# Building one-hot scatter matrices as 32-bit words in a graph propagation kernel

## The chip, the cores and the metric

The kernel runs on one core of a Trainium2 chip. The metric is the device time of one execution in microseconds (us), and the time of a kernel is the median of its runs. The engines are PE (matrix products, with its weight loads as PEld), DVE (elementwise work and reductions), ACT (copies and functions), POOL (here mostly gathers by index) and SP (which issues most of the copies between memory and the on-chip buffers).

## The reference

`x` has N = 10000 rows of D = 128 floats. There are E = 160000 edges with a source and a destination node each. Seven times, each node's row becomes the sum over its incoming edges of the source's row, with two factors per edge:

```python
h = x
toks = [x]
for _ in range(K):                                   # K = 7 hops
    msg = h[src] * deg_inv_sqrt[src, None] * deg_inv_sqrt[dst, None]
    h = _segment_sum(msg, dst, N)
    toks.append(h)
```

The eight rows of a node are then the tokens of one attention block (layer norm, attention with `wq`, `wk`, `wv`, `wo`, a residual and a softmax readout with `w_r`), which gives one row per node.

## The kernel before, in words

**How a hop is computed.** The nodes are cut into 79 blocks of 128 destinations. For each block the edges are placed in slots, and a hop is two matrix products with one-hot matrices: a *gather* product picks the source rows of the slots out of a table in SBUF, and a *scatter* product adds the slots up into the 128 destinations. The matrices of a block lie in one fp8 tile `w` of 128 partitions by (19 + 18) x 128 columns. Its first 19 x 128 = 2432 columns are the scatter half: 19 groups of 128 slots, where the column of the slot's destination has a 1. Its last 18 x 128 = 2304 columns are the gather half. The matrices are the same in all seven hops. They are made once, during hop 1, used there, and stored to memory (`gsd`); hops 2 to 7 load them again.

**The stages.** First all edges are read and ranked by counting with one-hot matrices (`pass_a`, `decode`). Then comes hop 1, which works on 20 *quads* of four blocks (the last has three). Around it run three generators: `place` for the next quad, `matrices` for this one, and `hop1` (with `block`) for the quad before. Then follow hops 2 to 7 (L654 to L705), and the attention at the end. Before the attention a count decides whether a slow path is needed.

**`place` (L371 to L457).** It handles a quad in two pairs of blocks. For each pair DVE makes a one-hot tile `oh` (L195, called at L379; two buffers), PE sums it up (`ur`, L383), ACT copies, PE adds prefixes (L389), and `rank` makes the product `ux` on DVE (L208), has PE sum it (L212, L213) and reduces to `rk` (L216). From `rk` come `rob` (L195, at L394) and two tiles `R` (L201), and PE multiplies `oh` and `R` to the slot table `tb` (L402), which ACT copies to `tbs`. DVE then makes `vo` and its largest values `ov` (L405, L407). After both pairs the table's source rows are written to memory as `srow` (L412), and the destinations come back, through small products (L416), as `dsl`: one number per partition, block and slot group, which is 1 plus the destination within the block, or 0 where a slot is empty (L420, an ACT copy from PSUM into f16). Some ten small integer instructions, two one-hot tiles `ohp` (L446), PE's products of them (L449), `lo` (L452), `oidx` (L455) and `Sov` (L456) deal with edges that found no slot.

**`matrices` (L459 to L480).** For each block of a quad, `row` issues a copy of one row of `srow` to all partitions (`rb`, L464 to L466, one buffer, on SP). DVE compares `rb` with the partition's number, which is the gather half (L473), and compares `dsl` with 1 to 128, which is the scatter half (L476): the `dsl` value is stretched over 128 columns, the numbers 1 to 128 (`iof1`, f16) over the 19 groups. The next row's copy is issued as soon as the gather half has read the buffer. Then SP stores `w` to `gsd` (L478). `w` comes from a pool of six buffers, so a new one has to wait until an earlier block's products have read theirs.

**`block` (L492 to L566).** For each pair of slot groups PE makes eight gather products (L541), ACT copies the result to an f16 tile `eb` (L544), and PE makes the scatter products into `acc` (L517). Two products take rows that POOL fetched by index (`og`, L488; products at L503, L530). At the end of a block DVE reduces `acc` to `s` (L532), copies the degree `indeg` (L595) and reduces `mx` (L597), ACT scales (L596, L571), and SP stores the token rows `tok` (L575).

**The order of the work.** In the hops each engine's instruction list is written by a scheduler that plans with costs of its own and moves instructions of the three generators past each other; on the chip each engine then runs its list strictly in order and waits for semaphores. So a change of one instruction can move others. The attention is scheduled by hand.

Of the kernel before, what the change touches and what calls it, by code (L numbers as in the profile page):

```python
# [7 lines left out]
F32 = mybir.dt.float32  # L8
F16 = mybir.dt.float16
BF16 = mybir.dt.bfloat16  # L10
F8 = mybir.dt.float8e4
I32 = mybir.dt.int32
AF = mybir.ActivationFunctionType
ALU = mybir.AluOpType
# [15 lines left out]
NJ = NG + NI  # L30
# [7 lines left out]
class Hops:  # L38
# [332 lines left out]
    def place(self, ts, got):  # L371

        tc, nc, V, A, T, G = self.tc, self.nc, self.nc.vector, self.nc.scalar, self.nc.tensor, self.nc.gpsimd
        wp, w1, n = self.bwp, self.bw1, len(ts)
# [34 lines left out]
        n, a, b = len(ts), ts[0], ts[-1] + 1  # L409
        msc = self.psm.tile([128, 128], F32, name="msc")  # L410

        nc.sync.dma_start(self.srow[a:b, :].rearrange("t (s r) -> s t r", r=CAP), tbs[:4 * NG, :n, 0:CAP])  # L412
        dsl = wp.tile([128, 4, NJ], F16, name="dsl")
        for g in range(n):
            for q in range(4):
                T.matmul(msc[32 * q:32 * q + 32, 32 + g * NJ:32 + (g + 1) * NJ], tbs[:, g, CAP:2 * CAP], self.esel[:, q, :],  # L416
                         start=True, stop=True, tile_position=(0, 32 * q))
                T.matmul(msc[32 * q:32 * q + 32, 16 + g * NI:16 + (g + 1) * NI], tbs[:, g, 0:CAP], self.esel[:, q, NG:],
                         start=True, stop=True, tile_position=(0, 32 * q))
        A.copy(dsl[:, :n, :], msc[:, 32:32 + n * NJ].rearrange("p (g j) -> p g j", j=NJ))  # L420
        V.tensor_scalar(self.oidx[:, a:b, :NI], msc[:, 16:16 + n * NI].rearrange("p (g i) -> p g i", i=NI), -1.0, 0.0, op0=ALU.add, op1=ALU.max)
        got.append(dsl)
        n = 4
# [30 lines left out]
        n = len(ts)  # L454
# [4 lines left out]
    def matrices(self, ts, dsl, W):  # L459

        nc, V = self.nc, self.nc.vector

        def row(t):
            rb = self.bw1.tile([128, 4 * NG * CAP], F16, name="rb")  # L464
            r1 = self.srow[t:t + 1, :]
            nc.sync.dma_start(rb, bass.AP(tensor=r1.tensor, offset=r1.offset, ap=[[0, 128], [1, 4 * NG * CAP]]))  # L466
            return rb

        rb = row(ts[0])
        yield  # L470
        for g, t in enumerate(ts):
            w = self.gsp.tile([128, (NJ + NG) * 128], F8, name="w")
            V.tensor_scalar(w[:, NJ * 128:], rb, self.pid1, None, op0=ALU.is_equal, saturate=False)  # L473
            if t != ts[-1]:
                rb = row(t + 1)
            V.tensor_tensor(w[:, :NJ * 128].rearrange("p (j d) -> p j d", d=128), dsl[:, g, :, None].to_broadcast([128, NJ, 128]),  # L476
                            self.iof1[:, None, :].to_broadcast([128, NJ, 128]), op=ALU.is_equal, saturate=False)
            nc.sync.dma_start(self.GSd[t], w)  # L478
            W.append(w)
            yield  # L480
# [728 lines left out]
```

## Time and profile before

| what | value |
|---|---|
| runs | 3994.35, 3999.09, 4004.58 us; median 3999.09 us |
| span of the profiled execution | 3993.2 us |
| PE busy | 3698.2 us (93%) |
| DVE busy | 3307.4 us (83%) |
| ACT busy | 2652.0 us (66%) |
| POOL busy | 1775.7 us (44%) |
| scatter half, L476 on DVE | 79 instructions, 211.7 us |
| gather half, L473 on DVE | 79 instructions, 111.9 us |

The span runs from the first to the last instruction of one profiled execution; the times of the runs also hold what lies around it, 5.9 us by the median. A busy PE is not PE at its peak, since matmuls are pipelined and their recorded ends are modelled. DVE instructions overlap a little in the records too. The profile has a view of groups of instructions by line and shape (count, total busy time, mean), one of waits (who waited for whom, total, times, longest), a timeline of single instructions, and windows, which give the busy time of each engine in a stretch of the span.

### The profile page before, as it was taken

The page shows a single profiled execution, that of the slowest core. Times are in us where ns is not written, and L with a number is a line of the kernel's source. Part 1 is how long each engine was busy: PE and PEld are TensorE (multiplying, and loading weights), DVE is VectorE, ACT ScalarE, POOL GpSimd, SP SyncE. Part 2 cuts the span into 40 slices and gives each one's busy share as a digit, 9 for nine tenths or more (in the row PEclk, how much of TensorE's full clock was granted, in tenths as well). Part 3 has the DMA queues.
Part 4 walks back from the last instruction along what each step waited for, and adds up shares of the span by engine and source line. Part 5 has one row for each costly group of instructions (what it writes and reads, how often), then busy time and mean ns, then how long its engine had stood idle before and what let it go on. Part 6 is the DMA issues. An engine that isn't in the chain of part 4 may idle for free. (4 is left out here: it accounts for less than half of the span.)

```text
span 3993.2 us, 164299 instructions
## 1 busy us (share of the span) xinstructions
PE 3698.2 (93%) x69691; PEld 3031.4 (76%) x69691; DVE 3307.4 (83%) x6948; ACT 2652.0 (66%) x6799; POOL 1775.7 (44%) x2355
## 2 busy tenths in 40 slices
PE   4776799999979999999999999999999997999997
PEld 3765666667648888888888888888888886888875
DVE  8998999999967777777777777777766665999998
ACT  6774366666666666666666666666655557888884
POOL 0000333333326665666666666666656661222222
PEclk8988999999989999999999999999999998999998
DMA  3100444444456666666666666666656653222220
GB/s 107 30 1 1 129 152 153 146 153 149 145 179 198 201 200 196 202 202 203 192 203 203 195 201 201 202 199 203 203 182 187 188 168 91 76 78 78 75 74 13
DMA packets 320622, 594.87 MB, mean 149 GB/s; under 512 B 55623, under 2 KB 213541, under 8 KB 314629
## 3 DMA queue, kind: packets, MB, share of 16 engines
q1 hardware_dynamic: 219749, 477.37, 38.5%
q0 software_dynamic: 35392, 72.55, 6.0%
q10 hardware_dynamic: 64736, 34.38, 3.0%
q8 instruction: 546, 8.95, 0.9%
q14 instruction: 199, 1.63, 0.1%
HBM read 455.43 MB, written 128.67 MB: 146 GB/s over the span
## 5 line engine op out<-in xcount | busy, mean ns | idle before, releaser
L544 ACT CAST eb<-p 128x512 f16<-128x512 f32 x3081 | 1591.0, 602 | 694.6 <-PE p L541 670.7
L544 DVE CAST eb<-p 128x512 f16<-128x512 f32 x1896 | 1179.3, 683 | 346.7 <-PE p L541 331.1
L541 PE MATMUL p<-tab,w 128*32 128x256 f16 x39816 | 1284.9, 274 | 39.8 <-ACT eb L544 22.1
L517 PE MATMUL acc<-eb,w 128*128 128x256 f16 (+1 forms) x9954 | 1239.8, 273 | 12.7 <-DVE indeg L595 10.3
L541 PEld LDWEIGHTS <-w 128*32 128x32 fp8e4 x39816 | 1001.3, 96 | 240.1 <-issue 181.6
L517 PEld LDWEIGHTS <-w 128*128 128x128 fp8e4 x9954 | 953.1, 98 | 174.5 <-issue 61.6
L488 POOL DMA_INDIRECT og<-tabh,oidx x553 | 638.4, 1154 | 732.4 <-DVE vi L440 400.6
L488 POOL DMA_INDIRECT og<-tabd,oidx x541 | 563.3, 1041 | 433.8 <-PE acc L530 268.3
L573 POOL TENSOR_SCALAR r<-s,ctok 128x128 f32<-128x128 f32 x474 | 296.1, 625 | 33.6 <-DVE s L532 18.5
L678 DVE SCALAR_TENSOR_TENSOR tab<-s,c,tab 128x128 f16<-128x128 f32 x395 | 139.2, 352 | 183.1 <-ACT tab L677 182.1
L677 ACT ACTIVATE tab<-s,c 128x128 f16<-128x128 f32 x395 | 158.5, 401 | 182.7 <-DVE s L532 182.4
L487 POOL COPY og<-eb 128x1 f16<-128x1 f16 x457 | 85.1, 186 | 426.7 <-ACT eb L544 426.6
L315 ACT ACTIVATE o<-oh,d2s 128x79 f16<-128x79 f16 x800 | 204.7, 373 | 80.9 <-PE ta L329 80.9
L532 DVE TENSOR_REDUCE s<-acc 128x128 f32<-128x256 f32 x553 | 228.5, 413 | 27.4 <-PE acc L530 20.4
L918 ACT ACTIVATE junk<-x 128x128 f32<-128x128 f32 x625 | 245.0, 394 | 0.0
L476 DVE TENSOR_TENSOR w<-dsl,iof 128x2432 fp8e4<-128x2432 f16 x79 | 211.7, 2679 | 0.0
L976 POOL TENSOR_TENSOR p<-e,in 128x512 f32<-128x512 f32 (+1 forms) x40 | 40.8, 1021 | 342.8 <-DVE e L974 342.8
L904 PEld LDWEIGHTS po<-v,pT 128*128 128x128 f32 x1250 | 159.0, 193 | 44.7 <-issue 27.6
L329 PE MATMUL ta<-o,ro 128*128 128x158 f16 x1250 | 119.7, 267 | 77.9 <-DVE ro L325 77.8
L893 PE MATMUL pv<-Wv,xT 128*128 128x131 f32 x1250 | 175.7, 284 | 4.5 <-ACT xT L873 3.8
L329 PEld LDWEIGHTS <-ro 128*128 128x128 f16 x1250 | 114.5, 113 | 82.2 <-DVE ro L325 82.0
L904 PE MATMUL po<-v,pT 128*128 128x128 f32 x1250 | 166.8, 277 | 7.7 <-DVE o L910 7.7
(277 smaller groups left out, 4642.3 us busy)
## 6 DMA issues: line engine op xcount, KB each, us to landing
w<-gsd SPq DMA_DIRECT2D x474, 592.0 KB
gsd<-w SPq DMA_DIRECT2D x79, 592.0 KB
rb<-srow SPq DMA_DIRECT2D x79, 576.0 KB
tok<-r SPq DMA_DIRECT2D x546, 64.0 KB
x<-tok SPq DMA_DIRECT2D x266, 128.0 KB
tabd<-tab ACTq DMA_DIRECT2D x395, 64.0 KB
og<-tabh,oidx POOLq DMA_INDIRECT x553
og<-tabd,oidx POOLq DMA_INDIRECT x541
```

The source lines that it names most:

```text
L315: A.activation(o[:, j - a, NK:, i], oh[:, j, :, i], AF.Copy, scale=d2s[:, c0:c0 + 1])
L329: T.matmul(ta, ro[:, j - a, :, i], o[:, j - a, :, i], start=j + i == 0, stop=j + i == NP)
L476: V.tensor_tensor(w[:, :NJ * 128].rearrange("p (j d) -> p j d", d=128), dsl[:, g, :, None].to_broadcast([128, NJ, 128]), self.iof1[:, None ...
L488: self.nc.gpsimd.indirect_dma_start(out=o, out_offset=None, in_=src[0] if i == NI else src[1], in_offset=bass.IndirectOffsetOnAxis(ap=self ...
L517: T.matmul(acc[0][:, :m], w[:, J * 128:(J + 1) * 128], e[:, j, :m], start=first and J == 0, stop=J == NG - 1 and not (first or late))
L532: V.tensor_reduce(s, acc[0][:, 0:256].rearrange("p (h d) -> p d h", h=2), axis=X, op=ALU.add)
L541: T.matmul(p[32 * q:32 * q + 32, j], w[:, NJ * 128 + s * CAP:NJ * 128 + (s + 1) * CAP], tab[:, s, :], start=True, stop=True)
L544: (A.copy if evac(jj) else V.tensor_copy)(e[:, :n, 0:256], p[:, :n].rearrange("p j h d -> p j (h d)"))
L573: self.nc.gpsimd.tensor_scalar(r, s, ct[:, t:t + 1], None, op0=ALU.mult)
L893: T.matmul(p[:, g - a, :], S[i]["xT"][:, g, :], Wv, start=True, stop=True)
L904: T.matmul(p[:, g - a, :], PT[i % 2][:, g, :], S[i]["v"][:, g, :128], start=True, stop=True)
L918: A.activation(j, S[i]["x"][:, g, :], AF.Square, bias=S[i]["x"][:, g, 0:1], scale=-1.0, accum_out=S[i]["sq"][:, g:g + 1])
```

## The change

The scatter half is written as 32-bit words that hold four fp8 columns each. The destination number d (0 to 127, or -1 for an empty slot) is split into a word number d >> 2 and a byte number d & 3. Once for each quad, three small integer instructions make, from `dsl`, an integer `byte` whose bits are those of the float 56 x 2^(8 x byte number), and the word number; then one compare of the word numbers with 0 to 31 gives an fp8 tile `hit` for all four blocks. For each block, one product of `hit` (1.0 or 0) with the float in `byte`, written as an integer, gives the 608 words of the scatter half: 56 is 0x38, which is 1.0 in fp8, and the power of 2 puts it into its byte. `dsl` becomes an int32 tile, and ACT takes 1 off while it copies. The lines below L471 move down by 3 to 8, so that the old L473, L476 and L478 are L481, L484 and L486 of the changed kernel, and L532 is L540.

```diff
-        dsl = wp.tile([128, 4, NJ], F16, name="dsl")
+        dsl = wp.tile([128, 4, NJ], I32, name="dsl")
...
-        A.copy(dsl[:, :n, :], msc[:, 32:32 + n * NJ].rearrange("p (g j) -> p g j", j=NJ))
+        A.activation(dsl[:, :n, :], msc[:, 32:32 + n * NJ].rearrange("p (g j) -> p g j", j=NJ), AF.Copy, bias=-1.0)
...
         rb = row(ts[0])
         yield
+        n = len(ts)
+        byte = self.bw1.tile([128, 4, NJ], I32, name="byte")
+        V.tensor_scalar(byte[:, :n], dsl[:, :n], 3, 26, op0=ALU.bitwise_and, op1=ALU.logical_shift_left)
+        V.tensor_single_scalar(byte[:, :n], byte[:, :n], 0x42600000, op=ALU.bitwise_or)
+        V.tensor_single_scalar(dsl[:, :n], dsl[:, :n], 2, op=ALU.arith_shift_right)
+        hit = self.bw1.tile([128, 4, NJ, 32], F8, name="hit")
+        V.tensor_tensor(hit[:, :n], dsl[:, :n, :, None].to_broadcast([128, n, NJ, 32]),
+                        self.iof[:, None, None, :32].to_broadcast([128, n, NJ, 32]), op=ALU.is_equal, saturate=False)
         for g, t in enumerate(ts):
             w = self.gsp.tile([128, (NJ + NG) * 128], F8, name="w")
             V.tensor_scalar(w[:, NJ * 128:], rb, self.pid1, None, op0=ALU.is_equal, saturate=False)
             if t != ts[-1]:
                 rb = row(t + 1)
-            V.tensor_tensor(w[:, :NJ * 128].rearrange("p (j d) -> p j d", d=128), dsl[:, g, :, None].to_broadcast([128, NJ, 128]),
-                            self.iof1[:, None, :].to_broadcast([128, NJ, 128]), op=ALU.is_equal, saturate=False)
+            V.tensor_tensor(w[:, :NJ * 128].bitcast(I32).rearrange("p (j d) -> p j d", d=32), hit[:, g],
+                            byte.bitcast(F32)[:, g, :, None].to_broadcast([128, NJ, 32]), op=ALU.mult)
             nc.sync.dma_start(self.GSd[t], w)
```

In the changed program the scheduler also puts other instructions of hop 1 in another order on all engines but POOL; after hop 1 the order is the same.

## The prediction

> **What bounds the kernel now.** I read the windows first: they say which engine fills which stage. The columns are the stretch, its length, then busy time and instructions of PE, PE's weight loads, DVE, ACT and POOL, the granted clock, and DMA.
>
> ```profile
> core 0: us, PE busy (x) PEld busy (x) DVE busy (x) ACT busy (x) POOL busy (x), PEclk, DMA share, GB/s
> 500.00:1100.00 600.00, 557.55 (x10074) 415.10 (x10066) 593.52 (x876) 370.81 (x812) 221.97 (x127) 1.00 0.48 150
> 1100.00:1165.00 65.00, 59.33 (x1067) 39.79 (x1055) 44.36 (x77) 49.54 (x107) 20.89 (x15) 1.00 0.45 138
> 1165.00:3300.00 2135.00, 2095.50 (x43632) 1763.25 (x43630) 1580.45 (x3249) 1374.94 (x2775) 1321.30 (x1889) 0.99 0.64 197
> ```
>
> The reader is to see that in hop 1 (about 415 to 1165 us), where the matrices are made, DVE is busy 593.5 of 600 us, while in the later hops PE is full (2095 of 2135) and DVE is not. The edited lines run in hop 1 alone. The instructions of all engines after it stand in the same order in the changed program, so I take the later 2800 us as unchanged. The chain of waits follows the attention at the end only and says nothing of hop 1. DVE's own waits and the edited line's row come next:
>
> ```profile
> DVE w L473 <- DMA rb<-srow: 7.7, 11, 1.9
> DVE s L532 <- PE acc L530: 4.4, 1, 4.4
> ```
> ```profile
> L476 DVE TENSOR_TENSOR w<-dsl,iof x79: 2669/2680/2687, 415.5 to 1139.0; 128x2432 fp8e4<-128x2432 f16 x79
> ```
>
> DVE hardly waits (7.7 us for the copied rows, over 11 times), so time taken off it should shorten the stage. 78 steps in 723.5 us are 9.28 us a block, **37.1 us a quad** of four blocks.
>
> **The DVE work.** Rows of the list of groups by shape, out<-in, count, total and mean ns:
>
> ```profile
> L476 DVE TENSOR_TENSOR w<-dsl,iof 128x2432 fp8e4<-128x2432 f16 x79 | 211.7, 2679 | 0.0
> ...
> L456 DVE TENSOR_TENSOR Sov<-lo,iof 128x512 fp8e4<-128x512 f32 x19 | 13.0, 683 | 0.0
> ...
> L440 DVE TENSOR_SCALAR vi<-vi 128x32 int32<-128x32 int32 x20 | 3.8, 191 | 0.0
> ...
> L351 DVE SCALAR_TENSOR_TENSOR kB<-t 128x2000 f16<-128x2000 int32 x1 | 2.2, 2231 | 0.0
> ...
> L276 DVE TENSOR_TENSOR it<-it 128x1250 int32<-128x1250 int32 x1 | 1.4, 1449 | 0.0
> ```
>
> and the timeline of DVE (start, duration), from the middle of the stage:
>
> ```profile
> 800.34 0.17 DVE L452 COPY lo<-msc 128x12 f32<-128x12 f32 x1
> ...
> 801.32 0.16 DVE L455 SCALAR_TENSOR_TENSOR oidx<-lo 128x4 int32<-128x4 f32 x1
> 801.40 0.68 DVE L456 TENSOR_TENSOR Sov<-lo,iof 128x512 fp8e4<-128x512 f32 x1
> 802.00 0.98 DVE L201 TENSOR_TENSOR R<-rob,dl 128x1600 f16<-128x1600 f16 x1
> ...
> 802.90 1.41 DVE L473 TENSOR_SCALAR w<-rb,pid 128x2304 fp8e4<-128x2304 f16 x1
> ...
> 804.23 0.41 DVE L532 TENSOR_REDUCE s<-acc 128x128 f32<-128x256 f32 x1
> 804.57 0.15 DVE L595 COPY indeg<-acc 128x1 f32<-128x1 f32 x1
> 804.63 0.20 DVE L405 SCALAR_TENSOR_TENSOR vo<-rk,TT 128x50 f32<-128x50 f16 x1
> ...
> 811.56 2.13 DVE L208 TENSOR_TENSOR ux<-oh,U 128x3800 f16<-128x3800 f16 x1
> ...
> 813.61 0.28 DVE L597 TENSOR_REDUCE mx<-tab 128x1 f32<-128x128 f32 x1
> ...
> 813.80 2.68 DVE L476 TENSOR_TENSOR w<-dsl,iof 128x2432 fp8e4<-128x2432 f16 x1
> ...
> 816.40 0.41 DVE L216 TENSOR_REDUCE rk<-ur 128x50 f16<-128x250 f32 x1
> 816.73 1.41 DVE L473 TENSOR_SCALAR w<-rb,pid 128x2304 fp8e4<-128x2304 f16 x1
> ```
>
> Each instruction starts about 0.08 us before the recorded end of the one ahead. So what one costs is start to start: the old compare 816.40 - 813.80 = 2.60 us, Sov 802.00 - 801.40 = 0.60 us, the gather half (L473) 1.33 us. The slope between the two compares is (2.60 - 0.60) / 1920 = 1.04 ns an element.
>
> Removed: 79 x 2.60 = 205.4 us. Added:
> - the compare of word numbers, 2432 elements, once a quad: 19 x 2.60, and 1.97 for the last quad's 1824, 51.4 us. It reads int32 where the old one read f16; L276 and L351 read int32 at 1.16 and 1.12 ns an element, close to L476's 1.10, so I take the same rate.
> - the product, 608 words a block: 0.60 + 96 x 1.04 ns = 0.70 us, x79 = 55.3 us. No row reads fp8 or writes int32 from two tensors. Nearest is Sov (4 bytes in, 1 byte out). From below 0.35 us, two words a step, as L473's 0.6 ns an element would have it; from above 1.33 us, two steps a word. I take 0.70, since every two-tensor row with a stretched operand moves one element a step.
> - three small integer instructions a quad on 76 words: 0.19 less 0.08, plus 44 more at about 1.1 ns, 0.16 us; 60 x 0.16 = 9.6 us.
>
> Together 116.3 us, so DVE is relieved of **89 us, 4.45 us a quad**. The wider dsl copy on ACT and its bias I cost at nothing: ACT is busy 371 of 600 us, and it is the same one instruction a quad.
>
> One rule of the Trainium skill would turn the sign. "VectorE: DVE Perf Modes", section "The perf-mode tier table", has two-tensor instructions on 16-bit data at twice the fp32 rate. The old f16 compare would then take about 1.4 us and the change would add some 10 us. The L476 row at 1.10 ns an element refutes that here: its stretched operands get no such mode.
>
> **What becomes late.** The built order of the changed program puts less between the gather halves W0 to W3 of a quad. Each W waits for rb, and rb has one buffer, so its copy starts only when the W before has ended. That round trip, from the end of one W to a W that had to wait:
>
> ```profile
> rb<-srow SPq DMA_DIRECT2D x79, 576.0 KB
> ```
> ```profile
> 884.93 1.42 DVE L473 TENSOR_SCALAR w<-rb,pid 128x2304 fp8e4<-128x2304 f16 x1 [0.44 <-DMA rb<-srow]
> 892.26 1.42 DVE L473 TENSOR_SCALAR w<-rb,pid 128x2304 fp8e4<-128x2304 f16 x1 [0.35 <-DMA rb<-srow]
> ```
> ```profile
> 1130.97 1.47 DVE L473 TENSOR_SCALAR w<-rb,pid 128x2304 fp8e4<-128x2304 f16 x1 [0.33 <-DMA rb<-srow]
> ...
> 1137.16 1.42 DVE L473 TENSOR_SCALAR w<-rb,pid 128x2304 fp8e4<-128x2304 f16 x1 [0.92 <-DMA rb<-srow]
> ...
> 1144.00 1.42 DVE L473 TENSOR_SCALAR w<-rb,pid 128x2304 fp8e4<-128x2304 f16 x1 [1.88 <-DMA rb<-srow]
> ```
>
> is 5.91 (892.26 - 886.35), 4.72 and 5.42 us. The ones that nobody waited for were shorter than their gaps, so I take 4.9, near the lowest. The new gaps, start to start: W0 to W1 holds lo 0.08, a product 0.70, oidx 0.08, Sov 0.60, s 0.34, indeg 0.06, ux 2.05 and mx 0.19, together 4.10: **wait 0.8**. W1 to W2 holds two products, rk 0.33, three of R's kind (0.90), s, indeg, mx and vo 0.12: 5.14, wait 0.1 from the spread. W2 to W3: two maxima 0.18, oh and ux 2.05 each, s and indeg: 4.68, wait 0.1, as oh before it can wait too. SP's queue holds a token store ahead of each rb, whose sum s comes 2 us or more before the W that frees rb, so I cost it at nothing. The store of the finished w (to gsd) stands behind rb.
>
> The other new wait is at oh (L195), which the order now puts one pair earlier: it takes the buffer that the table products of PE (L402) still read.
>
> ```profile
> 806.93 1.81 PE L383 MATMUL ur<-oh,id 128*128 128x152 f16 x25
> ```
> ```profile
> 791.93 1.86 PE L212 MATMUL ur<-ux,id 128*128 128x250 f16 x16
> ...
> 796.75 0.84 PE L541 MATMUL p<-tab,w 128*32 128x256 f16 x24
> ...
> 797.52 0.84 PE L517 MATMUL acc<-eb,w 128*128 128x257 f16 x6
> 798.29 0.62 PE L541 MATMUL p<-tab,w 128*32 128x256 f16 x16
> 798.85 0.62 PE L517 MATMUL acc<-eb,w 128*128 128x257 f16 x4
> ...
> 803.04 2.00 PE L402 MATMUL tb<-R,oh 128*76 128x64 f16 x50 [0.29 <-DVE R L201]
> ```
>
> R ends at 802.98 and these products at 805.04, 2.06 us later. Behind the second pair's R the new order has only the maxima and eight small instructions (about 0.1 each) before oh, 0.9 us from R's recorded end: **wait 1.1 a quad**. The first pair has a W and more between: nothing.
>
> New waits 2.1 us a quad, old ones gone 7.7 / 20 = 0.4: net 1.7. So 4.45 - 1.7 = 2.75 us a quad, x20 = **55 us**.
>
> PE is next. Per quad: 288 gathers at (0.84 - 0.62) / 8 = 0.028 us, 7.9; 72 scatters at 0.11, 7.9; L383, L212 and L402 twice each, 11.3; the rest about 3: 30 of the 34.4 us that are left. It does not bound over a quad, but waits can arise where DVE leads it.
>
> The profiled execution spans 3993.2 us, the median of the runs is 3999.1, so 5.9 lies around it. 3993.2 - 55 + 5.9 = **3944**.
>
> **The rivals.**
> 1. The whole relief arrives: rb returns within the gaps and oh finds its buffer free, 4.45 + 0.4 = 4.85 a quad, 97 us: 3902. For it: most round trips in the trace were not waited for. Against: the 4.72 is already over two of the gaps. The Trainium skill, "DMA: Bandwidth & Descriptors", section "Anatomy of one DMA — SWDGE (gpsimd) path", has 2.0 us plus the bytes at 436 GB/s, an estimate of 3.4 us for these 576 KB, by which no W would wait; the rows here that waited all show more.
> 2. rb at its upper rows: at 5.4 us the three gaps wait 1.3, 0.3 and 0.7; with oh 3.4, net 3.0, 1.45 a quad left: 3970.
> 3. **Slower**: the same round trip longer still, as the store of w now follows W0 by 0.7 us where the old compare kept it 2.6 behind, beside the next copy. Each further us costs 3 a quad; the gain is gone where it passes 5.9 us, and at 6.5 the kernel is at about 4035. For it: the 5.91. Against: the stores are queued behind the copy.
> 4. The change does not do what it says: the product takes two steps a word, 0.63 x 79 = 50 us back: 3994, no change. If the compare did so too, another 50: slower.
>
> **How the numbers follow.** Forecast 0.58, rival 1 0.14, rival 2 0.12, rival 3 0.10, rival 4 0.06. A measurement of this kernel tells about 0.3%, 12 us, from no change. Forecast and rivals 1 and 2 are faster, 0.84; rival 4 is the same, 0.06; rival 3 slower, 0.10. The range takes in forecast and rivals 1 and 2, 3902 to 3975.
>
> **What would show it.** Line for line: products of 0.78 us recorded and compares of 2.68; DVE busy about 85 us less up to the end of hop 1; hop 1 ending near 1110 instead of 1165; waits for rb of some 20 us in all and for PE's table products at oh of some 20. If products record 1.4 us, rival 4 holds; if rb's waits pass 50 us, rival 3; if DVE waits for PE's other results, PE's order is the bound that I left out.

## The result and the profile after

| | before | after |
|---|---|---|
| median of the runs | 4001.0 us (4 runs, 3994.4 to 4004.6) | 3964.2 us (4 runs, 3957.6 to 3965.8) |
| span of the profiled execution | 3993.2 us | 3963.6 us |
| last degree copy, end of hop 1 | 1165.6 us | 1130.4 us |

The changed kernel takes 0.9908 of the time before (95% interval 0.9894 to 0.9922), some 37 us less. The forecast was 55 less (3944), and 3964 lies inside the range. The sign and the place came out, and so did the relief of DVE and its new waits. A third of the gain did not, and what bounds the stage after the change was not foreseen.

The two windows of hop 1, each up to the kernel's own last degree copy, first of the kernel before, then of the changed one (columns as in the prediction: window, length, busy time and count of PE, PEld, DVE, ACT and POOL, PE's granted clock, DMA share, GB/s):

```profile
415.00:1165.60 750.60, 684.56 (x12288) 505.36 (x12287) 720.82 (x1067) 457.16 (x998) 277.75 (x160) 0.99 0.48 149
```
```profile
415.00:1130.40 715.40, 671.20 (x12295) 493.15 (x12292) 639.47 (x1152) 455.58 (x998) 248.78 (x160) 0.99 0.50 157
...
500.00:1100.00 600.00, 570.72 (x10544) 422.12 (x10544) 552.37 (x991) 388.16 (x854) 204.69 (x134) 1.00 0.51 161
```

Hop 1 is 35.2 us shorter (750.6 - 715.4). DVE is busy 81.3 us less (720.8 - 639.5), but it now stands still for 75.9 us where it stood for 29.8: 46.1 us of the relief became waiting. In the stretch that the prediction quoted for the kernel before, DVE has gone from 593.5 to 552.4 of 600 us and PE from 557.6 to 570.7: the fuller engine is now PE. The rest of the program is 5.6 us longer in this profiled execution (2833.2 against 2827.6 us), which is why the spans differ by 29.6 only. In the variants of the changed kernel below it took from 2827.0 us (e1_rb2) to 2834.0 us (e5_tail), so this much is scatter between executions and not a cost of the edit.

The edited lines, in the list of groups by shape of the changed kernel (count, total us, mean ns, idle time before):

```profile
L481 DVE TENSOR_SCALAR w<-rb,pid 128x2304 fp8e4<-128x2304 f16 x79 | 111.9, 1417 | 25.2 <-DMA rb<-srow 25.0
L484 DVE TENSOR_TENSOR w<-hit,byte 128x608 int32<-128x608 fp8e4 x79 | 61.9, 784 | 0.4 <-PE acc L536 0.2
L477 DVE TENSOR_TENSOR hit<-dsl,iof 128x2432 fp8e4<-128x2432 int32 x19 | 51.0, 2683 | 0.0
L473 DVE TENSOR_SCALAR byte<-dsl 128x76 int32<-128x76 int32 x19 | 5.6, 297 | 0.0
L474 DVE TENSOR_SCALAR byte<-byte 128x76 int32<-128x76 int32 x19 | 3.8, 200 | 0.5
L475 DVE TENSOR_SCALAR dsl<-dsl 128x76 int32<-128x76 int32 x19 | 3.7, 193 | 0.0
```

The product records 784 ns for 608 words and the compare 2683 ns, the two numbers that the prediction had named. So nothing of the loss lies in their prices. DVE's waits tell where it shows; first those of the kernel before over the whole stage, then those of the changed kernel (us in total, times, longest):

```profile
DVE s L532 <- PE acc L530: 11.9, 3, 4.4
...
DVE ux L208 <- ACT U L391: 0.7, 1, 0.7
```
```profile
DVE w L481 <- DMA rb<-srow: 25.0, 27, 3.7
DVE s L540 <- PE acc L538: 19.4, 5, 4.0
DVE oh L195 <- PE tb L402: 15.3, 24, 0.9
DVE ux L208 <- ACT U L391: 7.5, 11, 2.8
```

With the 7.7 us for `rb` that the prediction showed, the four lines grew by 17.3, 7.5, 15.3 and 6.8: together 46.9, where the new idle time is 46.1. The 15.3 and most of the 17.3 had been forecast. The wait for ACT's `U` had not, nor had the one at `s`. All five of the latter stand at the end of the stage (the timeline of the changed kernel, then that of the one before, in brackets the idle time ahead):

```profile
1101.89 1.42 DVE L481 TENSOR_SCALAR w<-rb,pid 128x2304 fp8e4<-128x2304 f16 x1 [3.66 <-DMA rb<-srow]
...
1113.88 0.42 DVE L540 TENSOR_REDUCE s<-acc 128x128 f32<-128x256 f32 x1 [3.97 <-PE acc L538]
...
1119.40 0.42 DVE L540 TENSOR_REDUCE s<-acc 128x128 f32<-128x256 f32 x1 [3.97 <-PE acc L538]
```
```profile
1144.00 1.42 DVE L473 TENSOR_SCALAR w<-rb,pid 128x2304 fp8e4<-128x2304 f16 x1 [1.88 <-DMA rb<-srow]
...
1165.57 0.15 DVE L595 COPY indeg<-acc 128x1 f32<-128x1 f32 x1
```

The last gather half starts 42.1 us earlier (1101.9 against 1144.0). From there to the last degree copy it is 28.5 us now and was 21.6: the last blocks come 5.52 us apart (1119.40 - 1113.88), as they did in the kernel before, and DVE waits for PE's products in each, so its new speed is of no use to them (the run e5_tail below looks at what sets this pace). Of the 42.1 us, 6.9 go back.

Last, the chain of waits of the changed kernel in one period in the middle of the stage (start, us, what):

```profile
791.52 1.82 DVE R L201 x2
...
793.39 2.03 PE tb L402 x50
...
795.44 2.14 DVE oh L195
...
801.58 1.65 PE ur L383 x25
803.23 0.55 PE p L549 x16
803.77 0.55 PE acc L525 x4
...
809.72 1.80 PE ur L212 x16
...
813.09 0.98 DVE rob L195
...
814.41 1.82 DVE R L201 x2
...
816.27 2.02 PE tb L402 x50
```

It passes from DVE to PE and back: DVE makes `R`, PE multiplies it, DVE may then write the next `oh`, and from 800 to 813 us the chain is PE working through its list, but for one ACT copy of 0.59 us. That suggested the theory below; a chain is only one path, so it took runs to show it.

### The profile page after: what moved, and what is told of

Its sections match the earlier page's. It is cut to its first block, busy times and chain, and to the rows that moved or that the text cites. A ratio compares the mean times of both kernels' runs of the same rounds, so it can differ in the third digit from the quotient of the medians.

```text
span 3963.6 us, 164425 instructions
## 1 busy us (share of the span) xinstructions
PE 3686.5 (93%) x69691; PEld 3021.7 (76%) x69691; DVE 3226.0 (81%) x7028; ACT 2650.2 (67%) x6799; POOL 1745.0 (44%) x2355
## 4 chain that ended last, share of the span: by engine, by line
PE 73%; DVE 16%; DMA 5%; ACT 2%; issue 2%; SPq 0%; ACTq 0%; POOL 0%; DVEq 0%; POOLq 0%
PE p L549 25%; PE acc L525 24%; PE acc L511 4%; PE pv L901 3%; PE po L912 3%; PE pu L890 3%; PE ta L329 2%; DMA rb<-srow 2%; DVE R L201 2%; PE pt L880 2%; DVE oh L195 2%; PE tb L402 1%; DVE w L481 1%; DVE ro L325 1%; DMA og<-tabd,oidx 1%
## 5 line engine op out<-in xcount | busy, mean ns | idle before, releaser
L496 POOL DMA_INDIRECT og<-tabh,oidx x553 | 585.9, 1059 | 597.3 <-DVE vi L440 401.8
L496 POOL DMA_INDIRECT og<-tabd,oidx x541 | 586.2, 1083 | 563.1 <-PE acc L538 404.6
L540 DVE TENSOR_REDUCE s<-acc 128x128 f32<-128x256 f32 x553 | 230.2, 416 | 37.0 <-PE acc L538 30.4
L901 PEld LDWEIGHTS pv<-Wv,xT 128*128 128x128 f32 x1250 | 153.4, 192 | 21.2 <-issue 8.2
```

Of the source, the lines that this page charges most:

```text
L496: self.nc.gpsimd.indirect_dma_start(out=o, out_offset=None, in_=src[0] if i == NI else src[1], in_offset=bass.IndirectOffsetOnAxis(ap=self ...
L540: V.tensor_reduce(s, acc[0][:, 0:256].rearrange("p (h d) -> p d h", h=2), axis=X, op=ALU.add)
L901: T.matmul(p[:, g - a, :], S[i]["xT"][:, g, :], Wv, start=True, stop=True)
```

## The experiments

Theory at the start: the waits that the prediction named (the one `rb` buffer, the `oh` buffer behind PE's table products) are what keeps the relief from arriving. Rival: they are only where DVE happens to stand, since PE or a chain through PE and DVE sets the pace; take one wait away and another takes its place. All ratios are against the kernel before, which ran again beside each group of variants (its medians are 3998.0 to 4001.0 us), with their 95% interval; the "end of hop 1" is the last degree copy of the profiled execution.

**A second `rb` buffer (e1_rb2).** The changed kernel, with every other row copy up to block 59 going to a part of the second table that hop 1 does not use yet.

```diff
-            rb = self.bw1.tile([128, 4 * NG * CAP], F16, name="rb")
+            rb = self.tab[1][:, 70:79, :].rearrange("p t w -> p (t w)") if t % 2 and t < 60 else \
+                self.bw1.tile([128, 4 * NG * CAP], F16, name="rb")
```

> The changed kernel, but the copied row rb has a second buffer for the odd blocks below 60 (15 of the 20 quads): a part of the second table that hop 1 writes only later. Theory (DVE paces hop 1, and what the relief lost went into DVE's new waits): the 25.0 us of DVE's waits for rb in the changed kernel fall to 9 or less, and hop 1's last degree copy comes 12 to 16 us earlier than 1130.4 us; the whole at about 3950, ratio to before 0.9875. Rival (PE and ACT set the pace, the waits are only where it shows): the waits for rb go, others grow by as much, and no more than 4 us are won, 3960 or above.

Measured: 3954.8 us, 0.9898 (0.9883 to 0.9914), hop 1 ending at 1125.0. DVE's waits between 500 and 1080 us, in the changed kernel and then in this one:

```profile
DVE w L481 <- DMA rb<-srow: 16.5, 21, 2.0
DVE oh L195 <- PE tb L402: 14.9, 23, 0.9
```
```profile
DVE oh L195 <- PE tb L402: 19.7, 25, 1.0
DVE ux L208 <- ACT U L391: 5.0, 5, 2.8
DVE w L482 <- DMA rb<-srow: 3.0, 4, 0.9
DVE w L482 <- PE acc L537: 2.4, 7, 0.3
DVE rk L216 <- PE ur L213: 1.7, 8, 0.2
```

The `rb` wait lost 13.5 of its 16.5 us, and hop 1 became 5.4 shorter. Waits for PE's results (the first, fourth and fifth of these lines) are 23.8 where the `oh` line had 14.9. More of the removed wait came back elsewhere than arrived; the intervals of this kernel and of the changed one overlap. The time lies between the two expectations (3950, and 3960 or above). The end of hop 1 came 5.4 us earlier where the theory asked for 12 to 16, so the rival is nearer to what happened in the stage.

**A third `oh` buffer (e2_oh3), and both (e3_both).** `oh` of every third pair, below block 44, goes to another unused part of that table; e3_both adds the edit of e1_rb2.

```diff
...
-            oh = self.onehot(wp, "oh", cols(self.kB), NS)
+            oh = self.onehot(wp, "oh", cols(self.kB), NS, 55 if (ts[0] + p0) // 2 % 3 == 2 and ts[0] < 44 else None)
```

> The changed kernel, but every third pair's one-hot tile oh lies in a third buffer for the quads below block 44 (11 of 20). Theory: DVE's waits at oh for PE's table products, 15.3 us in the changed kernel, fall to about 7, and the time by 8: 3956, ratio 0.9889. Rival: DVE waits as long elsewhere, 3962 or above.

> Both: the second buffer of rb and the third of oh. Theory: the two gains add, 20 to 24 us under the changed kernel, 3942, ratio 0.985. Rival: PE at 30 us a quad and ACT's copies hold hop 1, under 6 us won, 3958 or above.

Measured: e2_oh3 3968.0 us, 0.9924 (0.9910 to 0.9937), hop 1 to 1138.3; e3_both 3956.4 us, 0.9903 (0.9887 to 0.9918), to 1124.8. The third buffer gained nothing: from 500 to 1080 us the wait for PE's table products is still 14.4 us (12.7 at `oh`, 1.7 where `oh` lies in the table) against 14.9, and the one for `U` grew from 7.5 to 10.6. Together they are no better than e1_rb2 alone (3954.8). In e2_oh3 the rival holds, and in e3_both the time is just under the 3958 of the rival and far from 3942. The theory fails here: these waits are not a sum of costs that can be taken off one by one.

**The product made twice (e4_twice).** 79 more products, 55 us of DVE work, writing the same words again.

```diff
+            V.tensor_tensor(w[:, :NJ * 128].bitcast(I32).rearrange("p (j d) -> p j d", d=32), hit[:, g],
+                            byte.bitcast(F32)[:, g, :, None].to_broadcast([128, NJ, 32]), op=ALU.mult)
```

> The changed kernel, but the product that writes the words is made twice for each block: 79 more instructions of 0.70 us start to start, 55 us of DVE work. Theory: DVE still paces hop 1, so most of it shows: 55 less at most 15 that now pass while rb is on its way, 40 to 55 us more, 4004 to 4019, near the kernel before or over it. Rival (DVE has slack behind PE or ACT): under 20 us more, 3984 or below.

Measured: 3982.5 us, 0.9972 (0.9960 to 0.9985), hop 1 to 1150.5. The ratio rose by 0.0064, so 55 us of DVE work cost 26 us (15 to 36 by the ends of the two intervals); the end of hop 1 moved by 20. The time falls in the rival's range (3984 or below). So DVE no longer sets the pace alone.

From here on the theory was another one: **after the change PE's own work sets the pace, in a chain with DVE; before it, DVE did.** It asks for the same test on the other engine, and for both tests in the kernel before.

**PE work added to both kernels (e7_before_ur, e8_after_ur).** The 25 products of `ur` (L383) run a second time with the same values, 1.65 us for each of 40 pairs, 66 us, of which 63 come after 415 us.

```diff
-            for c in range(NCH):
+            for c in [*range(NCH), *range(NCH)]:
```

> The kernel before, but PE makes the 25 products of ur (L383) twice: 38 more groups of 1.65 us, 63 to 66 us of PE work in all. Theory (DVE paces hop 1 before the change, PE has slack): under 25 us more, 4025 or below. Rival (PE paces already before): 45 us or more.

> The same 63 to 66 us of PE work in the changed kernel. New theory (the change hands the pace over to a chain that runs through PE for most of a quad): 40 to 66 us more, 4004 or above. Rival (DVE still paces, with its new waits): under 25 us more, 3989 or below.

**DVE work added to the kernel before (e9_before_dve).** 79 compares of 608 elements ahead of the real one, into columns that it then overwrites, 55 us.

```diff
+            V.tensor_tensor(w[:, :NJ * 32].rearrange("p (j d) -> p j d", d=32), dsl[:, g, :, None].to_broadcast([128, NJ, 32]),
+                            self.iof1[:, None, :32].to_broadcast([128, NJ, 32]), op=ALU.is_equal, saturate=False)
```

> The kernel before, with one more compare of 608 elements a block on DVE (overwritten by the old compare): 79 x 0.70 = 55 us of DVE work, as much as the doubled product added to the changed kernel, where it cost 18 to 25 us. Theory (DVE paces hop 1 before the change): 45 to 55 us more, 4046 or above. Rival (DVE was not the bound before either): 25 us or less.

Measured: e7_before_ur 4038.7 us, 1.0099 (1.0085 to 1.0113); e8_after_ur 4024.8, 1.0066 (1.0054 to 1.0078); e9_before_dve 4066.9, 1.0171 (1.0158 to 1.0185). As us of about 4000, over the kernel that was edited, and in brackets how much later hop 1 ended:

| work added | to the kernel before | to the changed kernel |
|---|---|---|
| 55 us on DVE | +68 (+66), e9_before_dve | +26 (+20), e4_twice |
| 66 us on PE | +40 (+43), e7_before_ur | +63 (+62), e8_after_ur |

One window from the middle of the stage (500 to 1080 us) for six kernels, in this order: before, after, before with DVE work, after with DVE work, before with PE work, after with PE work.

```profile
500.00:1080.00 580.00, 538.98 (x9735) 401.57 (x9727) 573.52 (x843) 358.67 (x785) 216.28 (x123) 1.00 0.48 152
```
```profile
500.00:1080.00 580.00, 552.37 (x10192) 410.16 (x10192) 538.18 (x954) 372.88 (x821) 195.42 (x128) 1.00 0.52 161
```
```profile
500.00:1080.00 580.00, 521.27 (x8982) 381.64 (x8981) 569.00 (x837) 327.57 (x721) 241.43 (x114) 0.96 0.43 139
```
```profile
500.00:1080.00 580.00, 552.48 (x10004) 404.91 (x10001) 559.50 (x996) 366.56 (x806) 257.75 (x125) 0.99 0.46 153
```
```profile
500.00:1080.00 580.00, 551.62 (x9981) 421.26 (x9978) 557.16 (x804) 341.79 (x746) 251.93 (x117) 0.99 0.45 145
```
```profile
500.00:1080.00 580.00, 562.17 (x10162) 424.32 (x10158) 503.59 (x891) 340.60 (x756) 173.74 (x119) 1.00 0.46 148
```

The first number after the length is PE's busy time, the third DVE's. Before the change DVE is at 573.5 of 580, and work added to it is paid in full and more, while of the added PE work 40% costs nothing. That is less slack than expected: +40 misses the theory (under 25) and lies nearer to the rival (45 or more), so PE was close to the pace already. e9_before_dve and e8_after_ur came out as the theory had it. After the change it is the other way about: PE's 66 us cost 63 and lift it to 562.2 while DVE sinks to 503.6, and DVE's 55 us cost under half. Most of the pace has passed from one engine to the other. It has not passed altogether: the +26 and the +40 say that in each kernel the second engine is close behind. Each variant also has a new order, which by itself moved two kernels by 10 or 11 us (the last experiment below); the DVE row turns by 42 us, well clear of that, and the PE row by 23, which is less so. The direction is shown, its exact size is not. Why DVE's 55 us cost 68 in the kernel before stays open; PE's granted clock is 0.96 in this window where the others have 0.99 or 1.00, and the order is another one.

**The last blocks (e5_tail).** From block 74 on DVE takes four of the nine copies of `eb` from ACT.

```diff
-                    yield from self.block(t, w, self.tab[0], og, pend, 2, (2, 2, 2, 3), True, lambda jj: True, fin1, t == 0)
+                    yield from self.block(t, w, self.tab[0], og, pend, 2, (2, 2, 2, 3), True, lambda jj, t=t: t < 74 or jj in (0, 2, 4, 5, 7), fin1, t == 0)
```

> The changed kernel, but in the last five blocks of hop 1 DVE makes four of the nine casts of eb, which ACT makes alone elsewhere. Theory: after the last gather half (1101.9 us in the changed kernel) hop 1 runs at ACT's pace, 5.5 us a block (nine casts of about 0.5, two copies of 0.4), and DVE is idle; with the casts shared the five blocks take about 4.4 us each, so 4 to 6 us less, 3959. Rival (PE sets that pace): no more than 1 us.

Measured: 3965.7 us, 0.9915 (0.9902 to 0.9927), hop 1 to 1129.8, 0.6 earlier than without. The last blocks come 5.15 us apart instead of 5.52, though they begin 1.5 us later (a sum at 1104.8 instead of 1103.2), and in them DVE's copies now wait for PE:

```profile
1112.03 1.29 DVE L552 CAST eb<-p 128x512 f16<-128x512 f32 x2 [1.13 <-PE p L549]
```

The expected gain of 4 to 6 us did not come. With ACT relieved a block takes 0.4 us less, so ACT's copies held it back by that much, and after that DVE's copies stand waiting for PE's products.

**One compare a block (e6_split).** The compare of word numbers for each block instead of once for four.

```diff
-        V.tensor_tensor(hit[:, :n], dsl[:, :n, :, None].to_broadcast([128, n, NJ, 32]),
-                        self.iof[:, None, None, :32].to_broadcast([128, n, NJ, 32]), op=ALU.is_equal, saturate=False)
...
+            V.tensor_tensor(hit[:, g], dsl[:, g, :, None].to_broadcast([128, NJ, 32]),
+                            self.iof[:, None, :32].to_broadcast([128, NJ, 32]), op=ALU.is_equal, saturate=False)
```

> The changed kernel, but the compare of word numbers is made for each block alone (608 elements) in place of once for four: 79 x 0.70 in place of 51 us, 4 us more of DVE work and 59 instructions more. If PE's work sets the pace after the change, this costs next to nothing, 3960 to 3970. Rival (DVE's work still tells, at the price that the change itself paid, 35 us for 89): 2 us, the same; only if the single compare is what the gain came from would it be 3980 or more.

Measured: 3965.5 us, 0.9914 (0.9900 to 0.9928), hop 1 to 1133.0. It can't be told from the changed kernel: that the compare is shared by four blocks is worth nothing that shows here, so the gain is not owed to the sharing.

**Fewer changes on PE (e10_runs3, e11_before_runs3, e12_rb2_runs3).** Gathers and scatters of a block in three runs of three pairs instead of 2, 2, 2 and 3, in the changed kernel, in the kernel before, and with the second `rb` buffer.

```diff
-                    yield from self.block(t, w, self.tab[0], og, pend, 2, (2, 2, 2, 3), True, lambda jj: True, fin1, t == 0)
+                    yield from self.block(t, w, self.tab[0], og, pend, 2, (3, 3, 3), True, lambda jj: True, fin1, t == 0)
```

> The changed kernel, but hop 1 makes a block's gathers in runs of three pairs of slot groups (3, 3, 3) in place of (2, 2, 2, 3), so that PE goes over between gather and other products 657 times instead of 781. In the changed kernel's trace each such step costs PE 0.11 us beyond the products (16 gathers 0.56 us start to start where the 4 column passes take 0.44). Theory (PE's own work paces hop 1 now): 124 x 0.11 = 14 us less, 10 to 18, about 3950. Rival (waits between the engines pace it, whatever PE's work): within 4 us of 3964.

> The same runs of three in the kernel before, where DVE paces: PE's steps between gather and other products fall from 705 to 633, 8 us of PE work. Theory: within 4 us of the kernel before. Rival (PE's work counts there as well): 8 us less or more.

> The changed kernel with the second buffer of rb and the runs of three: a version that may beat both. Theory: the gain of the runs (10 to 18 us, 677 steps in place of 797) comes on top of the 4 to 9 us of the second buffer, 3938 to 3950. Rival: the two overlap, 3950 to 3955.

Measured: e10_runs3 3972.6 us, 0.9934 (0.9921 to 0.9947); e11_before_runs3 4010.2, 1.0028 (1.0019 to 1.0037); e12_rb2_runs3 3954.4, 0.9890 (0.9874 to 0.9906). PE's busy time does sink in e10_runs3, over the whole of hop 1 from 671.2 to 663.7 us, half of the 14 us that had been expected. But PE then waits where it did not. First the window of e10_runs3 and that of e11_before_runs3, 500 to 1080 us; then PE's waits in the same stretch, after and e10_runs3:

```profile
500.00:1080.00 580.00, 539.61 (x10069) 412.29 (x10068) 532.97 (x946) 366.57 (x811) 233.40 (x128) 1.00 0.49 157
```
```profile
500.00:1080.00 580.00, 543.92 (x9508) 407.46 (x9507) 561.78 (x828) 344.97 (x765) 280.92 (x120) 0.94 0.45 148
```

```profile
PE tb L402 <- DVE R L201: 15.2, 29, 1.4
PE ur L212 <- DVE ux L208: 6.2, 14, 0.7
```
```profile
PE ur L212 <- DVE ux L208: 18.1, 15, 2.4
PE msc L449 <- DVE ohp L195: 7.1, 17, 0.7
```

With 657 changes between gathers and other products instead of 781, e10_runs3 was to gain, and e11_before_runs3 to stay as it was. By the ratios both are 10 or 11 us slower than the kernels they were made from, so both expectations failed, and their rivals too. For e10_runs3 the intervals just touch. In e11_before_runs3 PE's granted clock is 0.94 where the kernel before has 1.00 in this stretch, which may account for its loss. The new grouping also moves the scheduler's order, and these kernels do not part the causes, so whether fewer changes on PE can be turned into time is open. e12_rb2_runs3 is the lowest time measured (3954.4), in the rival's range and level with e1_rb2; its interval overlaps that of the changed kernel, so a gain over it is likely and not certain.

## Why the prediction was right, and where its size was off

- **What bounds hop 1 before: right.** DVE at 593.5 of 600 us set the pace; e9_before_dve, with 55 us added and 68 paid, shows it directly. That PE stood close behind (e7_before_ur, +40) was not seen.
- **The price of the edit: right to 10%.** Forecast 89 us of relief, recorded 81.3. The compare and the product came out as named, and so did the three small instructions: they record 297, 200 and 193 ns, and less the overlap of 0.08 us each that is 0.45 us a quad, where 0.48 had been put. So the missing 8 us lie in no edited row. About 4 of them are likely overlap that was lost, since an instruction before which DVE stands idle starts only after the recorded end of the one ahead: DVE's waits in hop 1 went from 26 to 76, and 50 x 0.08 us is 4.0, an estimate. The rest is spread over other rows. Rival 4 (two steps a word) falls by the 784 ns.
- **Why a word takes one step: wrong, and partly luck.** The prediction's reason, "every two-tensor row with a stretched operand moves one element a step", does not hold of the rows shown there. `R` (1600 elements, 0.98 us) and `ux` (3800, 2.13 us) have stretched operands too, and their slope is 1.15 / 2200 = 0.52 ns an element, two elements a step. They are f16 throughout, and their stretch leaves the last two elements side by side; L476 writes fp8 and repeats one value 128 times. Which of the two keeps L476 at 1.04 ns no run shows, so that row refutes no rule for data that is 16-bit throughout, and the price of the product came out without the reason that was given for it.
- **The new waits: nearly right.** 1.7 us a quad net, 34 in all; `rb` and `oh` grew by 17.3 and 15.3, together 32.6. The closeness of the sum is partly luck: 20 and 22 had been put for them, and 25.0 and 15.3 were measured. The 6.8 at `ux` were not priced: a moved order also brings DVE sooner to ACT's results. Rival 1, that the whole relief arrives, falls: the copied rows were waited for 27 times. The Trainium skill, "DMA: Bandwidth & Descriptors", section "Anatomy of one DMA — SWDGE (gpsimd) path", from which 3.4 us had been estimated for the copy, would have no such wait; the measurement decides. That section is about copies issued by gpsimd, and these are issued on SP, so its figure is not refuted for its own path. Rival 2's time, 3970, is nearer to the measured 3964 than the forecast is, but its mechanism did not come: it needs 2.3 us of waits for `rb` a quad, 46 in all, and 25.0 were measured. Rival 3 falls as well, at 25.0 us of such waits instead of more than 50.
- **"It does not bound over a quad": this step failed.** The prediction gave PE 30 of 34.4 us a quad, by products at their price inside a run of their kind, 0.028 us a gather. The changed kernel's PE timeline (start, duration) has

```profile
803.15 0.62 PE L549 MATMUL p<-tab,w 128*32 128x256 f16 x16
803.71 0.62 PE L525 MATMUL acc<-eb,w 128*128 128x257 f16 x4
804.16 0.17 PE L536 MATMUL acc<-ones,Sov 128*128 128x1 f16 x1
```

  and 16 gathers take 0.56 us from start to start (803.71 - 803.15), where 16 x 0.028 is 0.45: each change between weights of 128x32 and of 128x128 costs about 0.11 us more. The way back costs the same: in the prediction's rows 6 scatters take 0.77 us (798.29 - 797.52), where 6 x 0.11 is 0.66. The changed kernel's trace has 782 such changes in hop 1 (724 before, where the expectation of e11_before_runs3 has 705): 39 a quad and 4.3 us, so that PE needs 30 + 4.3 = 34.3. One quad from the middle of the stage, from its first gather half to that of the next, shows the same:

```profile
803.87:839.53 35.66, 34.31 (x635) 25.46 (x634) 33.35 (x60) 23.17 (x52) 11.89 (x8) 1.00 0.52 159
```

  PE is busy 34.31 of 35.66 us in it. The Trainium skill, "TensorEngine Tiling (Array Packing)", section "Key Properties", says that a change of the tiling mode drains TensorE; the 0.11 us agrees with it, though no run shows that a drain is the cause. The same could have been read from the row that the prediction itself shows: 557.6 of 600 us busy, times 37.1, is 34.5 us a quad, just the 34.4 that the forecast left. With PE that full, little of DVE's lead can be used: by the runs above, added PE work now counts nearly in full (63 of 66 us).
- **"x20": this failed too, by 6.9 us.** All 20 quads were taken alike, but behind the last matrices DVE has nothing left to make, and PE's products with ACT's copies, 5.52 us a block, set the pace there before and after.
- **The sum.** 55 forecast; less 8 for the relief as recorded, less 5 for the waits of the steady quads (39.4 against 34), less 7.5 for the waits at `s` at the end: 35, the 35.2 measured in hop 1. As DVE's time is busy or idle, this sum has to close; what made DVE idle is told by the added work, and not by the names of the waits. The medians differ by 7.2 us more than the spans (36.8 against 29.6): the changed kernel's profiled execution has 1.9 us around its span (3965.5 - 3963.6) where 5.9 were taken (every run on record has 1.7 to 2.2, so the other 4 of the 5.9 were a profiled execution faster than the median), it lies 1.3 above its median, and the median of before is 1.9 higher with the fourth run.

What stays open: which links of the chain between PE and DVE hold in each order that the scheduler writes. Every variant changes the order, and no run here held it fixed.

## What to carry to other kernels

Price a relief of the pacing engine only down to what the next engine needs per period, and read that need from its busy share of the period (557.6 of 600 here), or at least check it against a sum of instructions at their price inside a run of their kind. To learn which engine paces a stage, add the same work to one engine at a time in both kernels: the cost of the added work told here what three removed waits had not. Take the end of a stage by itself, since the last period has other work in it.

## What the runs showed that was not expected

A change on PE between gathers (weights of 128x32) and other products costs about 0.11 us, 4.3 us a quad, and the kernel that makes fewer of them was slower nevertheless, by 8 us in the medians (e10_runs3, 3972.6 against 3964.2; the intervals of the ratios just touch). Added DVE work of 55 us cost 68 us in the kernel before. Two prices that the prediction could only assume are now measured. An fp8 x f32 product written as integers takes 784 ns for 608 words, as a compare of 608 f16 numbers does (e9_before_dve, 781 ns):

```profile
L476 DVE TENSOR_TENSOR w<-dsl,iof 128x608 fp8e4<-128x608 f16 x79 | 61.7, 781 | 0.0
```

The compare of 2432 int32 numbers takes 2683 ns, where that of as many f16 numbers took 2679.
